# Low weight parts on VectorE, first clips on GpSimd, and the last third products by token halves

## The chip, the core and the metric

The kernel runs on one core of a Trainium2 chip. The metric is the device time of one execution in microseconds (us); lower is better. The engines of the core are named as in the profile: PE is TensorE (matmul), PEld its weight loads, DVE is VectorE, ACT is ScalarE, POOL is GpSimd and SP is SyncE, which only issues DMAs. Each engine takes its own instructions in the order in which the program has them, and waits where a semaphore tells it to.

## The reference

A Mamba-2 scan (batch 4, 8 heads, 768 steps, head dimension 32, state 16) is followed by a SiLU feed-forward block on its output, seen as 3072 tokens of 256 features. With `a` clipped to [1e-6, 1]:

```
for each chunk of 32 steps:            # per batch and head
    cum = cumsum(log a);  L = tril(exp(cum_i - cum_j))
    y   = ((C B^T) * L) x  +  (C state) * exp(cum)
    state = exp(sum log a) * state + sum_j exp(cum_last - cum_j) B_j x_j^T
X = y as (3072, 256)
h = X @ w_in                            # 256 x 2048
out = (h * sigmoid(h)) @ w_out          # 2048 x 256
```

`x`, `a`, `B`, `C` are float32; `w_in` and `w_out` arrive as float64.

## The kernel before

**Units and pairs.** The 3072 tokens are cut into 12 units `u` of 256 tokens (three to a batch), and these into 6 pairs `P` (in the first product `G`) of 512 tokens. The scan of a unit needs decay products (`E`, `P`: scans on DVE from factors that a DMA spreads over the partitions), `B` and `C` turned and weighted (`T`, `ce`, `B`, `C`), matmuls `g0` (C with B), `gd`/`D` (state updates), the mask `M` and the state steps `S` on DVE, `SM` on ACT, and the output matmuls `Y`. Its result is copied out of PSUM by ACT (`X0` for the first two units, `y` for the others).

**The feed-forward block.** Pair 0 uses float32 matmuls: `s` (first product), `si` (SiLU), `n` (second product, 32 of them). Pairs 1 to 5 use float32r, which rounds its operands, and so need three products: a high part `h`, a low part `l` and a third part `d` of both factors. `a` holds the `h` and `l` products of one block `i` of 256 features, `ax` rescales the sum in PSUM, `d` adds the third product, `dg` is the SiLU, `h`, `l`, `e` make the three parts of the result (ACT, DVE, DVE), and the second product takes them as single matmuls, the `f` items, from the list `S2`. Pair `P` has 8 blocks `i`, and per block 12 items: two halves `k`, two output halves `m`, three parts. The sums lie in four PSUM banks `ACC` (`h`+`l` and `d`, for `m` = 0 and 1).

**The weights** come as 16 blocks `n` of 256 columns (0 to 7 of `w_in`, 8 to 15 of `w_out`) as pairs of 32-bit words. ACT makes `u` (size of the high word) and `v` (low word), DVE clips `u` (`w,n,0`, line 292), shifts it (`w,n,1`, line 296) and sets the sign in `v` (`w,n,2`, line 299), POOL adds the two (`W`, line 310). Then come the parts: `H` on ACT (line 314), `Wl`, the low part, which POOL adds out of the high part and the weight (line 319), `Wd` on ACT (line 322), and `We`, an accumulating DMA on POOL's queue (line 326), which adds the low part into the third.

**The order of the work** is written out by hand: `SCHEDULE` is a list of tokens (`name,arguments`) that is emitted from left to right, and each engine gets its share in that order; `SLOTS` lists which buffer each request takes. `z` are matmuls on zeros at the start. The last pair is ended differently from the others: for its last blocks (`i >= LASTI`) the `m = 1` items are held back in `LAST`, `h` and `l` first, the third products (`d`) at the very end. Then `Vt` (line 703) adds the third products to the rest in four token blocks `k`, `ot` (line 715) turns them by matmuls on the identity, two blocks a half, `or` copies each half out of PSUM (ACT, DVE) and `os` (line 726) stores it.

Of the kernel before, what the change touches and what calls it, by code (L numbers as in the profile page):

```python
# [13 lines left out]
ALU = mybir.AluOpType  # L14
# [4 lines left out]
ip,0 ia cs ci ir,3 c1 ch c2 Ln,0,0,0,1 z,1 cI z,1 z,1 Lt,0,1,2,1 Lt,0,1,0,1 zr z,0,6 z,0,6 A z,0,6 z,1 cd lw,2 cP cp  # L19
Lt,0,1,1,1 z,1 z,1 PA,0 z,1 z,1 z,1 pb,0 Lt,0,1,3,1 ab,0,0 T,0,1 ab,0,1 P01,0 Ln,0,0,1,1 ab,1,1 Lx,0,0,0 lw,0 Lx,0,1,0  # L20
PA,1 ce,0,0 v,2 C,0 u,2 z,1 u,0 z,1 z,0,6 Ln,1,0,1,0 E,0,0 Ln,1,1,0,0 E,0,1 E,1,1 Ln,1,0,0,0 ce,0,1 w,0,0 B,0,0 z,0,6
B,0,1 z,0,6 Ln,1,1,1,0 tp,0 tq,0 D,0 g0,0 S,0,0 Lt,3,1,1,0 S,0,1 v,0 pb,1 w,2,0 S,0,2 Lx,1,0,0 M,0,1 M,0,0 Lx,1,1,0
ir,0 ab,1,0 ct co lw,1 w,2,1 w,2,2 SM,0,1 SM,0,0 B,1,1 tp,1 ce,1,1 tq,1 Y,0 ce,1,0 X0,0,0 S,0,3 X0,0,1 E,1,0 P01,1
lw,3 W,2,2,0 W,2,2,1 H,2 u,1 w,0,2 B,1,0 w,0,1 g0,1 v,1 lw,4 D,1 S,1,0 S,1,1 S,1,2 v,3 SM,1,0 M,1,0 s,0,2 M,1,1 w,1,0
SM,1,1 W,0,2,0 ir,1 w,1,2 lw,10 u,3 Lt,3,1,3,0 W,0,2,1 ir,2 w,1,1 s,0,0 si,0,0 C,1 u,4 S,1,3 w,3,0 W,1,2,0 lw,9 lw,8
v,4 w,3,2 W,1,2,1 w,3,1 Y,1 lw,11 X0,1,1 X0,1,0 u,10 s,0,1 w,4,0 Ln,2,1,1,0 H,0 s,1,2 Wl,2 w,4,2 AA,0 Ln,2,0,1,0
si,0,2 si,0,1 s,1,0 u,9 v,10 w,4,1 AD,4 w,9,0 Ln,2,0,0,0 W,3,1,0 w,10,0 v,9 W,4,1,0 si,1,2 H,3 s,1,1 si,1,1 u,8 s,1,4
H,4 si,1,0 Lt,3,1,2,0 v,8 Ln,2,1,0,0 s,0,4 Lx,2,0,0 w,10,1 lw,5 AA,1 v,11 ca La,2,0,0 w,9,1 tp,2 si,1,4 Wl,4 AD,0
w,8,0 w,8,1 w,8,2 Lt,3,1,0,0 La,2,1,0 w,10,2 lw,7 Lx,2,1,0 w,9,2 si,0,4 W,8,1,0 lw,6 w,11,2 W,9,1,0 Lp,2,0 W,10,1,0
u,5 s,1,3 AD,2 Lt,3,0,1,0 s,0,3 n,1 tq,2 si,1,3 H,8 AD,1 v,5 w,5,0 n,1 T,3,1 n,1 ce,2,0 La,3,1,0 E,2,1 La,3,0,0 ce,2,1  # L30
n,1 u,11 w,11,0 n,1 E,2,0 si,0,3 w,11,1 v,7 Wd,4 n,1 Wd,3 B,2 n,1 g0,2 gd,2 w,5,1 b,2,0 b,2,1 n,1 w,5,2 Lt,3,0,3,0 u,6
W,5,1,0 P,2 n,1 Lt,4,1,2,0 M,2,1 s,0,5 Wd,0 n,1 v,6 C,2 ce,3,0 Lt,3,0,2,0 Lt,4,1,0,0 H,1 S,2,0 S,2,1 u,7 w,6,0
Ln,3,0,1,0 W,11,1,0 S,2,2 n,1 H,9 SM,2,0 Lt,3,0,0,0 n,1 M,2,0 w,7,0 SM,2,1 w,7,2 lw,12 E,3,0 Ln,3,0,0,0 w,7,1 Wd,1
ce,3,1 si,0,5 Lt,4,1,3,0 E,3,1 T,3,0 Lx,3,0,0 Y,2 Lp,3,0 n,1 w,6,1 Lx,3,1,0 u,12 y,2,0 W,7,1,0 n,1 s,0,7 y,2,1 H,5
w,6,2 g0,3 w,12,0 B,3 si,0,7 gd,3 W,6,1,0 w,12,1 Lt,4,0,1,0 s,0,6 b,3,0 P,3 AD,3 Wd,2 n,1 M,3,1 Wl,0 lw,13 S,3,0 b,3,1
Wl,5 xh,2 si,0,6 S,3,1 v,12 Ln,4,0,1,0 lw,14 x,2,1 C,3 n,1 Lt,4,0,0,0 Ln,4,0,0,0 u,13 s,1,6 M,3,0 x,2,0 La,4,0,0
w,13,0 S,3,2 v,13 SM,3,0 SM,3,1 We,0 w,12,2 Lt,4,0,2,0 Y,3 si,1,6 y,3,0 La,4,1,0 y,3,1 xh,3 S,3,3 W,12,1,0 La,5,0,0
Wl,3 Lp,4,0 x,3,0 s,1,5 n,1 Wd,5 w,13,2 w,13,1 Lt,4,0,3,0 a,1,0 H,6 si,1,5 n,1 Lt,4,1,1,0 H,7 lw,15 H,12 Wd,8 H,11
H,10 Lx,4,0,0 s,1,7 x,3,1 W,13,1,0 E,4,1 v,14 T,4,1 P,4 Lx,5,0,0 n,1 T,4,0 ax,1,0 Lt,5,1,2,0 d,1,0 Wl,10 Lx,4,1,0
ce,4,0 n,1 Wd,6 C,4 E,4,0 Lx,5,1,0 ce,4,1 n,1 u,14 dg,1,0 w,14,0 g0,4 B,4 gd,4 w,14,2 Wl,11 n,1 b,4,0 M,4,1 b,4,1  # L40
S,4,0 We,2 Lt,5,1,1,0 u,15 S,4,1 S,4,2 w,14,1 h,1,0 SM,4,1 si,1,7 M,4,0 Lt,5,0,3,0 SM,4,0 v,15 Lt,5,1,0,0 e,1,0
La,5,1,0 n,1 Lt,5,1,3,0 W,14,1,0 Wl,9 S,4,3 Wl,1 n,1 Y,4 y,4,0 n,1 We,1 f,1 Lp,5,0 y,4,1 w,15,0 w,15,1 La,6,0,0 w,15,2
Wl,8 We,4 W,15,1,0 Lt,5,0,2,0 xh,4 Lt,5,0,1,0 a,1,2 Lx,6,1,0 Wl,12 a,1,1 n,2 La,6,1,0 ax,1,1 T,5,1 Lt,6,1,0,0 E,5,0
n,1 ce,5,1 n,1 Wd,9 x,4,1 Wd,10 l,1,0 d,1,1 Ln,5,0,0,0 ax,1,2 n,1 We,8 d,1,2 P,5 dg,1,1 H,15 n,1 x,4,0 dg,1,2 We,3 n,1
a,1,4 E,6,0 ce,5,0 a,1,3 H,13 We,9 f,1 Vn,1 H,14 h,1,1 Vn,0 Ln,5,0,1,0 We,10 Wd,11 f,1 E,5,1 f,1 ax,1,4 f,1 ax,1,3 f,2
Lt,6,1,2,0 Wl,14 Lt,5,0,0,0 d,1,4 f,1 d,1,3 T,5,0 f,1 h,1,2 C,5 Lt,6,1,1,0 f,1 Lt,6,0,2,0 f,1 Lt,6,1,3,0 e,1,1 dg,1,4
f,1 Lt,6,0,3,0 Lt,6,0,0,0 Lt,6,0,1,0 f,1 l,1,1 f,1 B,5 dg,1,3 g0,5 T,6,1 gd,5 Wd,7 f,1 M,5,1 We,5 ce,6,0 b,5,0 f,1
h,1,3 Ln,6,0,1,0 f,1 Ln,6,0,0,0 S,5,0 b,5,1 e,1,2 S,5,1 S,5,2 f,1 Wl,7 a,1,5 M,5,0 l,1,2 h,1,4 f,1 Lp,6,0 f,1 ax,1,5
f,1 Lt,7,1,2,0 f,3 Lt,7,1,0,0 P,6 l,1,3 e,1,3 d,1,5 o,0,0,2 f,1 SM,5,1 dg,1,5 f,1 Wl,6 f,1 Wd,12 ce,6,1 We,7 f,2 l,1,4
f,2 SM,5,0 Y,5 T,6,0 Lt,7,1,1,0 f,1 We,11 We,12 f,3 y,5,1 f,1 a,1,7 E,6,1 Lx,6,0,0 Lx,7,0,0 e,1,4 f,2 B,6 f,3  # L50
Ln,7,0,1,0 y,5,0 ax,1,7 f,1 h,1,5 We,6 xh,5 d,1,7 f,2 C,6 dg,1,7 o,0,1,2 f,1 Lt,7,0,2,0 f,1 Wl,15 Wd,15 gd,6
Lt,7,1,3,0 Lx,7,1,0 g0,6 f,2 M,6,1 x,5,0 Wd,14 Wl,13 f,1 x,5,1 f,2 b,6,0 b,6,1 f,1 h,1,7 M,6,0 f,1 l,1,7 a,2,1 ax,2,1
a,1,6 Wd,13 Lp,7,0 S,6,0 d,2,1 f,1 e,1,5 We,13 S,6,1 ax,1,6 f,1 l,1,5 Lt,7,0,1,0 dg,2,1 La,7,1,0 T,7,1 d,1,6 dg,1,6
ce,7,0 f,1 S,6,2 SM,6,0 f,2 Lt,7,0,0,0 SM,6,1 f,2 h,1,6 f,1 Y,6 l,1,6 La,8,0,0 S,6,3 Lt,8,1,0,0 f,3 y,6,0 f,1 e,1,6
O,0,0,2,0,0 ce,7,1 P,7 f,3 y,6,1 We,15 La,7,0,0 xh,6 f,1 O,0,1,2,0,0 Lt,7,0,3,0 a,2,0 f,1 a,2,3 f,2 h,2,1 We,14 f,1
ax,2,0 E,7,0 d,2,0 ax,2,3 f,4 e,1,7 La,8,1,0 Lt,8,1,3,0 f,4 dg,2,0 f,1 E,7,1 f,1 d,2,3 f,1 l,2,1 f,1 x,6,0 Lt,8,1,2,0
a,2,2 f,2 h,2,0 dg,2,3 Ln,7,0,0,0 ax,2,2 f,1 O,0,1,2,3,0 e,2,0 f,4 l,2,0 T,7,0 f,2 Lt,8,0,2,0 B,7 f,1 Va,1,0 f,1 d,2,2
Va,1,1 f,1 Vd,1,0 f,1 Vd,1,1 f,3 dg,2,2 Lt,8,0,3,0 f,1 g0,7 x,6,1 gd,7 b,7,0 f,2 b,7,1 Lt,8,1,1,0 f,1 e,2,1 h,2,2
M,7,0 S,7,0 S,7,1 Ln,8,0,1,0 f,1 S,7,2 f,1 M,7,1 f,1 Ln,8,0,0,0 Lt,8,0,1,0 a,2,4 Lx,8,1,0 ax,2,4 C,7 a,2,5 f,2 T,8,1
ax,2,5 f,1 d,2,4 S,7,3 l,2,2 d,2,5 Lp,8,0 dg,2,4 E,8,0 P,8 SM,7,1 f,1 dg,2,5 f,4 e,2,2 Lt,8,0,0,0 E,8,1 f,2  # L60
O,0,1,2,2,0 f,1 T,8,0 SM,7,0 Lt,9,1,1,0 f,1 Y,7 y,7,1 f,1 h,2,3 f,1 e,2,3 f,1 y,7,0 a,2,7 Lt,9,0,2,0 ax,2,7 a,2,6 f,1
ax,2,6 Lx,8,0,0 Lt,9,0,0,0 Lx,9,0,0 d,2,7 La,9,0,0 f,1 d,2,6 f,1 l,2,3 f,2 ce,8,1 La,9,1,0 f,1 h,2,4 f,2 E,9,1 l,2,4
xh,7 ce,8,0 f,2 dg,2,7 f,4 dg,2,6 f,1 e,2,4 f,1 B,8 f,2 Ln,9,0,0,0 f,1 g0,8 gd,8 f,1 b,8,0 x,7,0 f,2 M,8,1 Lp,9,0
M,8,0 f,1 x,7,1 C,8 f,1 o,1,0,2 f,1 o,1,1,2 O,0,0,2,2,0 b,8,1 Lt,9,0,3,0 S,8,0 Lt,9,1,0,0 a,3,1 f,2 Lt,9,1,3,0
Lt,9,1,2,0 f,1 h,2,5 S,8,1 T,9,1 ce,9,0 ax,3,1 f,1 a,3,0 f,1 e,2,5 ax,3,0 S,8,2 d,3,1 h,2,6 f,1 d,3,0 l,2,5 SM,8,1
Lt,10,1,0,0 dg,3,0 f,3 Lt,9,0,1,0 f,1 l,2,6 f,1 Lt,10,1,3,0 SM,8,0 f,1 e,2,6 E,9,0 P,9 f,1 O,0,0,2,3,0 dg,3,1 f,1
ce,9,1 f,2 Ln,9,0,1,0 Lt,10,1,2,0 f,1 Y,8 y,8,0 f,1 h,3,0 B,9 f,1 O,0,1,2,1,0 f,2 h,2,7 f,1 O,0,0,2,1,0 O,1,0,2,0,0
f,1 h,3,1 l,2,7 O,1,1,2,1,0 y,8,1 Lt,10,1,1,0 e,2,7 C,9 a,3,2 f,3 a,3,3 e,3,0 f,2 ax,3,2 T,10,1 f,1 d,3,2 O,1,1,2,2,0
La,10,1,0 f,2 ax,3,3 xh,8 d,3,3 f,3 l,3,0 x,8,1 f,1 Lp,10,0 Lt,11,1,3,0 f,1 Lx,10,0,0 Lx,9,1,0 f,1 T,9,0 La,10,0,0
dg,3,2 f,1 dg,3,3 f,2 O,1,0,2,3,0 Va,2,0 g0,9 gd,9 f,1 b,9,0 Ln,10,0,0,0 M,9,1 Lt,10,0,0,0 f,1 l,3,1 b,9,1 f,1 a,3,5  # L70
f,1 Lt,11,1,2,0 Va,2,1 f,1 S,9,0 Vd,2,0 M,9,0 f,2 O,1,1,2,0,0 ce,10,1 a,3,4 f,1 O,1,0,2,1,0 Vd,2,1 f,1 o,2,0,2 e,3,1
f,5 ax,3,5 Lt,11,1,0,0 f,1 S,9,1 E,10,1 E,10,0 ce,10,0 Lt,11,1,1,0 ax,3,4 f,1 O,1,1,2,3,0 S,9,2 h,3,3 d,3,4
Ln,10,0,1,0 SM,9,0 SM,9,1 x,8,0 f,1 dg,3,4 f,1 d,3,5 f,1 dg,3,5 O,1,0,2,2,0 f,1 Lt,10,0,2,0 f,5 h,3,2 Y,9 y,9,1
o,2,1,2 Lx,10,1,0 f,1 S,9,3 l,3,2 e,3,2 f,1 Lt,10,0,1,0 f,2 h,3,5 a,3,7 f,3 e,3,3 f,3 O,2,1,2,0,0 h,3,4 La,11,1,0 B,10
l,3,3 l,3,4 f,1 Lt,10,0,3,0 f,1 y,9,0 ax,3,7 d,3,7 T,10,0 f,3 xh,9 dg,3,7 f,2 x,9,0 f,1 Lt,11,0,1,0 f,2 g0,10 h,3,7
gd,10 O,2,0,2,1,0 f,1 b,10,0 f,1 l,3,5 M,10,0 P,10 x,9,1 b,10,1 M,10,1 f,3 S,10,0 f,1 O,2,1,2,2,0 C,10 f,1 a,3,6 a,4,1
# [30 lines left out]
    "raw": """  # L107
0 1 2 3 4 5 6 0 1 2 3 4 0 5 6 3 2 1 4 0 1 5 4 6 3 2 1 0 5 6 4""",
    "hp": """
0 1 2 0 1 2 0 1 2 1 0 2 2 1 0 2 1 2 0 1 2 0 1 1 1 1 1 1 1 2 0 1 0 2 1 2 0 1 2 0 1 2 0""",  # L110
}
PASSED = (0, 1, 2, 3, 4, 5, 6, 7, 8, 9, 10, 11, 12, 13, 14, 15,)
LASTI = 6
# [769 lines left out]
```

## Time and profile before

| | |
|---|---|
| median of 3 runs | 330.02 us (329.69 to 330.54) |
| profiled execution: its time | 329.56 us |
| its span (first to last instruction) | 327.5 us |
| PE busy | 321.0 us, 3081 matmuls |
| DVE busy | 238.4 us |
| ACT busy | 207.7 us |
| POOL busy | 90.2 us |
| granted PE clock, mean | 0.999 |

The span leaves out 2.06 us of the execution's own time. A matmul record is longer than the step from one matmul to the next, because matmuls are pipelined; the steps are told from the starts. Tokens can be followed in the trace one by one, since each engine's instructions come in the order of `SCHEDULE`.

### The profile page before, as it was taken

What the parts mean: (1) busy time and instruction counts of PE and PEld (TensorE: products, weight loads), DVE (VectorE), ACT (ScalarE), POOL (GpSimd) and SP (SyncE); (2) the same over time, 40 slices, a digit from 0 to 9 for tenths busy, and PEclk for the clock granted to TensorE, in tenths of its full rate; (3) what the DMA queues carried; (4) which work ended last, traced back from release to release, by engine and by line L of the source; (5) the groups of instructions that cost most, each with busy time, mean ns of one, the idle gap of its engine ahead of it and who ended that gap; (6) DMA issues with size and microseconds to landing.
All of it is one profiled execution on the core that took longest, in us unless ns stands there. A gap on an engine that the chain in (4) does not pass through costs nothing.

```text
span 327.5 us, 7562 instructions
## 1 busy us (share of the span) xinstructions
PE 321.0 (98%) x3081; PEld 244.3 (75%) x3081; DVE 238.4 (73%) x311; ACT 207.7 (63%) x321; POOL 90.2 (28%) x104
## 2 busy tenths in 40 slices
PE   8999999999999999999999999999999999999995
PEld 3588656665677777877878878878887888888883
DVE  4999999799996955789377769776567554266373
ACT  2888855696498478655566766745856464764441
POOL 6467847658967343210100101010010000000000
PEclk9999999999999999999999999999999999999999
DMA  7999785865888357421603253144001200003102
GB/s 182 167 337 216 201 200 120 207 150 131 149 152 153 57 123 139 103 42 40 139 18 58 69 109 57 47 73 82 2 0 22 38 0 2 0 9 63 18 0 64
DMA packets 95761, 30.64 MB, mean 94 GB/s; under 512 B 80280, under 2 KB 86936, under 8 KB 95728
## 3 DMA queue, kind: packets, MB, share of 16 engines
q1 hardware_dynamic: 90576, 25.38, 35.1%
q0 software_dynamic: 2480, 4.39, 7.4%
q10 hardware_dynamic: 2672, 0.39, 0.7%
q8 instruction: 24, 0.39, 0.5%
q14 instruction: 9, 0.07, 0.1%
HBM read 22.61 MB, written 3.34 MB: 79 GB/s over the span
## 4 chain that ended last, share of the span: by engine, by line
PE 88%; DMA 4%; DVE 4%; issue 1%; ACT 1%; SPq 1%; POOL 0%; DVEq 0%
PE hp L763 29%; PE ga L782 17%; PE gb L782 17%; PE o_ps L763 6%; PE hp L673 4%; PE hp L741 4%; DMA ac<-r4k 2%; PE ga L613 2%; PE ga L553 2%; DMA ab<-az 2%; PE ga L604 1%; PE o_ps L417 1%; PE hp L468 1%; PE gb L604 1%; PE ga L539 1%
## 5 line engine op out<-in xcount | busy, mean ns | idle before, releaser
L763 PE MATMUL hp<-r4k,s2k 128*128 128x512 f32 x400 | 113.3, 394 | 0.0
L763 PEld LDWEIGHTS hp<-r4k,s2k 128*128 128x128 f32 x400 | 74.3, 188 | 16.2 <-issue 0.6
L630 DVE SCALAR_TENSOR_TENSOR r4k<-r4k,r4k 128x1024 fp32r<-128x1024 f32 x40 | 49.1, 1230 | 31.5 <-ACT r4k L809 23.9
L782 PE MATMUL ga<-raw,s2k 128*128 128x512 f32 x240 | 63.0, 398 | 0.0
L633 DVE SCALAR_TENSOR_TENSOR r4k<-r4k,r4k 128x1024 fp32r<-128x1024 f32 x40 | 50.1, 1257 | 16.5 <-ACT r4k L809 10.3
L782 PE MATMUL gb<-raw,s2k 128*128 128x512 f32 x240 | 61.5, 392 | 0.0
L782 PEld LDWEIGHTS ga<-raw,s2k 128*128 128x128 f32 x240 | 44.6, 188 | 12.2 <-issue 1.4
L782 PEld LDWEIGHTS gb<-raw,s2k 128*128 128x128 f32 x240 | 44.8, 188 | 10.4 <-ACT gb L793 0.4
L809 ACT ACTIVATE r4k<-r4k 128x1024 fp32r<-128x1024 f32 x40 | 41.8, 1056 | 2.0 <-DVE r4k L633 1.0
L486 POOL TENSOR_TENSOR BT<-bn,ab 128x256 f32<-128x256 f32 x10 | 10.0, 1000 | 94.3 <-DVE ab L478 49.7
L793 ACT ACTIVATE gb<-gb 128x1024 f32<-128x1024 f32 x20 | 20.2, 1008 | 20.8 <-PE gb L782 20.8
L763 PE MATMUL o_ps<-r4k,s2k 128*128 128x512 f32 x80 | 30.9, 392 | 0.0
L478 DVE TENSOR_TENSOR_SCAN ab<-ab,diag 128x512 f32<-128x512 f32 x20 | 28.3, 1425 | 3.3 <-DMA ab<-az 3.3
L741 PE MATMUL hp<-r4k,s2k 128*128 128x512 f32 x64 | 30.2, 598 | 0.0
L803 ACT ACTIVATE r4k<-ga 128x1024 f32<-128x1024 f32 x20 | 20.5, 1026 | 15.1 <-PE ga L782 14.2
L673 PE MATMUL hp<-r4k,s2k 128*128 128x256 f32 x128 | 29.8, 383 | 0.0
L793 ACT ACTIVATE ga<-ga 128x1024 f32<-128x1024 f32 x20 | 20.2, 1009 | 15.1 <-PE ga L782 15.1
L310 POOL TENSOR_TENSOR s2k<-s2k,s2k 128x512 uint32<-128x512 uint32 (+1 forms) x19 | 23.9, 1266 | 17.7 <-DVE s2k L296 9.9
L673 PEld LDWEIGHTS hp<-r4k,s2k 128*128 128x128 f32 x128 | 23.8, 190 | 5.5 <-issue 1.9
L803 ACT ACTIVATE r4k<-gb 128x1024 f32<-128x1024 f32 x20 | 20.5, 1024 | 9.2 <-PE gb L782 7.4
L319 POOL TENSOR_TENSOR s2k<-s2k,s2k 128x512 fp32r<-128x512 f32 x16 | 23.9, 1538 | 3.8 <-ACT s2k L314 3.8
L741 PEld LDWEIGHTS hp<-r4k,s2k 128*128 128x128 f32 x64 | 11.8, 189 | 9.6 <-issue 7.9
(120 smaller groups left out, 396.6 us busy)
## 6 DMA issues: line engine op xcount, KB each, us to landing
ab<-az SPq DMA_DIRECT2D x20, 256.0 KB
raw<-in_moe_w_in_dram SPq DMA_DIRECT2D x8, 512.0 KB
raw<-in_moe_w_out_dram SPq DMA_DIRECT2D x8, 512.0 KB
s2k<-s2k POOLq DMA_DIRECT2D x16, 256.0 KB, 4.5
out_dram<-r4k SPq DMA_DIRECT2D x44, 64.0 KB
xt<-in_x_dram SPq DMA_DIRECT2D x20, 128.0 KB
pz<-ac SPq DMA_DIRECT2D x10, 130.0 KB
bn<-in_B_dram SPq DMA_DIRECT2D x20, 64.0 KB
```

The lines of the kernel that those rows point to most:

```text
L310: nc.gpsimd.tensor_tensor(out=dst[:, :, fs].bitcast(U32), in0=u[:, :, fs], in1=v[:, :, fs], op=ALU.add)
L319: nc.gpsimd.tensor_tensor(out=t, in0=f32(WK[n, "h"]), in1=WT[n], op=ALU.add)
L478: nc.vector.tensor_tensor_scan(out=o, data0=src, data1=diag.rearrange("p h t -> p (h t)"), initial=0.0, op0=ALU.mult, op1=ALU.add)
L630: nc.vector.scalar_tensor_tensor(out=l, in0=f32(h), scalar=BACK, in1=y, op0=ALU.mult, op1=ALU.add)
L633: nc.vector.scalar_tensor_tensor(out=d, in0=f32(h), scalar=-(BACK + 1.0), in1=y, op0=ALU.mult, op1=ALU.subtract)
L673: nc.tensor.matmul(out=hp[:, i], lhsT=WT[j][:, kc, 128 * i:128 * i + 128], rhs=XM[:, 2 * kc:2 * kc + 2, u], start=(kc == 0), stop=(kc == K ...
L741: nc.tensor.matmul(out=NP["o"][m], lhsT=WT[8 + f // 2][:, f % 2, 128 * m:128 * m + 128], rhs=GT[0, f // 2][:, f % 2], start=(f == 0), stop ...
L763: nc.tensor.matmul(out=ACC[P, 2 * (p == "d") + m], lhsT=WK[8 + f // 2, p][:, f % 2, 128 * m:128 * m + 128], rhs=rhs, start=(f == 0 and p ! ...
L782: nc.tensor.matmul(out=o, lhsT=WK[j, q][:, kc, 128 * i:128 * i + 128], rhs=xs[:, 2 * kc:2 * kc + 2], start=(start and q == "h" and kc == 0 ...
L793: nc.scalar.activation(t, t, AF.Copy, scale=1.0 + Z)
L803: nc.scalar.activation(g, t, AF.Silu, scale=BACK)
L809: nc.scalar.activation(t, GT[G, i], AF.Copy, scale=-LESS * Z)
```

## The change

- `Wl,n` is done by DVE for all 16 weight blocks (`BESIDE`), as a `scalar_tensor_tensor` with a factor of 1.0. POOL did it before.
- The clip `w,n,0` of weight blocks 0, 1 and 2 (`CLIPPED`) is done by POOL. DVE did it before and still does for the other 13.
- `LASTI` is 5: the `m = 1` items of the last three blocks of the last pair are held back, not those of the last two. Their third products run as matmuls of 256 tokens, not 512: first the six for one half of the tokens into a bank of `ga`, then the six for the other half into a bank of `gb` (`s2_late`). The sums of blocks 0 to 4 stay in `ACC`; `Vc` (ACT) copies them to SBUF, `Vb` (DVE) adds the `h`+`l` sum, and `Vt` adds the late bank of the half that it belongs to.
- `SCHEDULE` and `SLOTS` are written anew. The order of tokens shifts throughout by some places on each engine. ACT's dummy SiLU `ct` stands ahead of its other work, so one activation table is loaded where there were two.

```diff
 PASSED = (0, 1, 2, 3, 4, 5, 6, 7, 8, 9, 10, 11, 12, 13, 14, 15,)
-LASTI = 6
+LASTI = 5
+CLIPPED = (0,1,2,)
+BESIDE = (0,1,2,3,4,5,6,7,8,9,10,11,12,13,14,15,)
...
             if what == 0:
                 u = wu[n]
-                nc.vector.tensor_scalar(out=u, in0=u, scalar1=LEAST, scalar2=MOST, op0=ALU.max, op1=ALU.min)
+                engine = nc.gpsimd if n in CLIPPED else nc.vector
+                engine.tensor_scalar(out=u, in0=u, scalar1=LEAST, scalar2=MOST, op0=ALU.max, op1=ALU.min)
                 return
...
             t = WK[n, p] = small([128, 2, WF], FR)
-            nc.gpsimd.tensor_tensor(out=t, in0=f32(WK[n, "h"]), in1=WT[n], op=ALU.add)
+            if n in BESIDE:
+                nc.vector.scalar_tensor_tensor(out=t, in0=f32(WK[n, "h"]), scalar=1.0, in1=WT[n], op0=ALU.mult, op1=ALU.add)
+            else:
+                nc.gpsimd.tensor_tensor(out=t, in0=f32(WK[n, "h"]), in1=WT[n], op=ALU.add)
...
     def f_vt(P, m, k):
-        o, t = (v.rearrange("p (c k t) -> p k c t", c=2, k=4)[:, k] for v in (OUT[P][0][:, m], ACC[P, 2 + m]))
+        o = OUT[P][0][:, m].rearrange("p (c k t) -> p k c t", c=2, k=4)[:, k]
+        t = LATE[k // 2][:, 1, 0:256].rearrange("p (c k t) -> p k c t", c=2, k=2)[:, k % 2]
...
-                         start=(f == 0 and p != "l"), stop=(f == NF - 1 and p != "h"), skip_group_check=True)
+                         start=(f == 0 and p != "l"), skip_group_check=True,
+                         stop=(f == (2 * LASTI if (P, m, p) == (NPAIR - 1, 1, "d") else NF) - 1 and p != "h"))
+
+    def s2_late(P, i, k, half):
+        f = 2 * i + k
...
+        nc.tensor.matmul(out=LATE[half][:, 1, 0:256].rearrange("p (c t) -> p c t", c=2),
+                         lhsT=WK[8 + f // 2, "d"][:, f % 2, 128:256],
+                         rhs=DT[P, i][:, k].rearrange("p (c u t) -> p c u t", c=2, u=2)[:, :, half],
+                         start=(f == 2 * LASTI), stop=(f == NF - 1), skip_group_check=True)
...
+    def f_vc(P, m):
+        nc.scalar.activation(OUT[P][0][:, m], ACC[P, 2 + m], AF.Copy, scale=BACK)
+
+    def f_vb(P, m):
+        o = OUT[P][0][:, m]
+        nc.vector.scalar_tensor_tensor(out=o, in0=ACC[P, m], scalar=BACK * (1.0 + Z), in1=o, op0=ALU.mult, op1=ALU.add)
...
         S2.extend(items((0,), "hld"))
-        LAST.append((items((1,), "hl"), items((1,), "d")))
+        LAST.append((items((1,), "hl"), [[partial(s2_late, G, i, k, half) for k in range(2)] for half in range(2)]))
         if i == NF // 2 - 1:
-            for v in range(2):
+            for t in LAST:
+                S2.extend(t[0])
+            for half in range(2):
                 for t in LAST:
-                    S2.extend(t[v])
+                    S2.extend(t[1][half])
```

Token orders that the prediction speaks of (other tokens left out):

```
before: ... Y,0 X0,0,0 X0,0,1 ... g0,1 D,1 ...       ... y,3,0 y,3,1 xh,3 ... x,3,0 ... a,1,0 ... ax,1,0 ... d,1,0
after:  ... Y,0 D,1 X0,0,0 X0,0,1 ... g0,1 ...       ... y,3,0 y,3,1 v,14 xh,3 ... x,3,0 ... a,1,0 ... ax,1,0 ... d,1,0
before (end): Va,5,0 f,1 Vd,5,0 f,5 o,5,0,2 f,3 Va,5,1 f,4 Vt,5,1,0 Vt,5,1,1 ot,5,1,0 ... Vt,5,1,2 Vt,5,1,3 ot,5,1,1 ...
after (end):  Va,5,0 ... Vc,5,1 f,10 Vb,5,1 Vt,5,1,1 f,3 Vt,5,1,0 ... Vt,5,1,2 Vt,5,1,3 ot,5,1,0 ot,5,1,1 ...
```

## The prediction

> **What bounds the kernel now.** I read the page's busy line and the chain that ended last, then the busy time by windows of 5 us to find where PE is not full, then PE's, DVE's and POOL's timelines around those places.
>
> ```profile
> PE 321.0 (98%) x3081; PEld 244.3 (75%) x3081; DVE 238.4 (73%) x311; ACT 207.7 (63%) x321; POOL 90.2 (28%) x104
> ...
> PE 88%; DMA 4%; DVE 4%; issue 1%; ACT 1%; SPq 1%; POOL 0%; DVEq 0%
> ```
>
> PE sets the time. Since the change keeps PE's work, it can gain only where PE waits, at the head, or behind the last matmul. The windows (length, then busy time of PE, PEld, DVE, ACT, POOL, granted clock) show the waits:
>
> ```profile
> 10.00:15.00 5.00, 4.80 (x148) 3.18 (x152) 4.88 (x12) 3.80 (x10) 1.19 (x4) 1.00 0.86 119
> 15.00:20.00 5.00, 4.53 (x129) 3.70 (x116) 4.86 (x11) 4.06 (x11) 3.19 (x5) 1.00 1.03 322
> ...
> 60.00:65.00 5.00, 4.28 (x101) 3.32 (x100) 3.46 (x9) 2.82 (x8) 2.46 (x3) 1.00 0.72 162
> ```
>
> All other windows from 10 to 320 us have PE full. So 1.4 us are to be had there (0.2 + 0.47 + 0.72), and no more. The two larger ones on PE's timeline, with what released them:
>
> ```profile
> 16.29 0.43 PE L553 MATMUL ga<-ce,bh 32*64 32x128 f32 x4 [0.47 <-ACT r4k L643]
> ...
> 63.59 0.27 PE L613 MATMUL ga<-cw,sm 32*64 32x64 f32 x2 [0.72 <-ACT sm L591]
> ```
>
> The first is `g0,1` waiting for the copy `X0`; the second is the end of `Y,3` waiting for `SM,3`. ACT is named there, but `SM,3,0` started 0.04 us after DVE's `S,3,2` ended at 62.77, so DVE was late. Why, DVE's and POOL's timelines and POOL's group say:
>
> ```profile
> 55.75 3.42 DVE L458 TENSOR_TENSOR_SCAN pfx<-pz,one 128x260 f32<-128x260 f32 x1
> ```
> ```profile
> 56.09 2.51 POOL L319 TENSOR_TENSOR s2k<-s2k,s2k 128x512 fp32r<-128x512 f32 x2
> ```
> ```profile
> L319 POOL TENSOR_TENSOR s2k<-s2k,s2k 128x512 fp32r<-128x512 f32 x16 | 23.9, 1538 | 3.8 <-ACT s2k L314 3.8
> L292 DVE TENSOR_SCALAR s2k<-s2k 128x512 f32<-128x512 f32 x16 | 10.5, 659 | 0.2 <-ACT s2k L283 0.2
> ```
>
> The scan has a median of 0.69 us; it took 3.42 while two `Wl` adds ran on POOL. Summing every DVE instruction's excess over its usual duration gives 26.0 us, of which 9.6 lie mostly beside `Wl` (3.8 before 62 us) and 9.3 beside `W` (line 310). DVE is full to 60 us, so these count.
>
> **Part 1: `Wl` on DVE, three clips on POOL.** Nothing in this trace shows `Wl` on DVE. Its nearest row is DVE's line 633 on the same shape and types (128x512, float32r out of two float32 operands): 0.68 us. So DVE gets 16 x 0.68 = +10.9 and loses three undisturbed clips, 3 x 0.41 = -1.2: +9.7 of its own work, against 9.6 of stretch that should go with POOL's adds. In total a draw, so the places decide. POOL loses 23.9 and gets three clips at about 0.67 (line 429, a POOL operation with a scalar on 48x512).
>
> *The clips.* They add a wait: DVE's shift `w,2,1` now stands behind POOL's `w,2,0`, with `S,0,2`, `M,0` and so `Y,0` (0.41 to spare) queued behind it. In the trace of before `u,2` was there at 9.31 and POOL's `B,0,1` ended at 10.84; a clip of 0.67 behind it ends at 11.5, and DVE reaches the shift about 12.3: 0. At 1.0 each (two thirds of `Wl`'s 1.54, for one operand less), the dearer bound, it is still there at 11.9, but `PA,1`, which stands behind both clips, moves from 12.6 to 13.3 and with it `pb,1` and `P01,1`: up to +0.5. I take 0.
>
> *At `Y,3`.* The last thing that it needs was `S,3,2`, and is now `M,3,0`. By usual durations, DVE's own work up to it grows by 1.1 (five `Wl` for 3.4, less 1.2, less what is now behind it). With 3.8 of stretch saved it ends 2.7 earlier, near 60.1, and PE is there at about 61.7: the 0.72 go. They stay if less than 2.2 of the 3.8 are saved.
>
> *At `Y,4`.* DVE's own work up to `M,4,1` is now 3.9 longer than before up to `M,4,0`, which ended at 78.27 (seven `Wl` are ahead). Less 0.45 that DVE idled: 81.7 without any saving, 77.9 with 3.8. PE is there at 78.6 + 1.1 (matmuls that move ahead of it) - 0.35 - 0.72 + 0.4 = 79.0. No wait, with a margin of 1.1.
>
> *The order on ACT.* `xh,3` now stands behind `v,14`, whose step in the trace of before is 0.56 us. The chain `Y,3`, `y,3`, `xh,3`, `x,3,0`, `a,1,0` had no slack (`x,3,0` ended at 66.51, as `a,1,0` began). It loses 0.56, and gets 0.22 back because `x,3,0` took 0.90 beside a `Wl` and should take 0.68: between 0 (if `v,14` finds a gap, since `Y,3`'s halves are copied apart) and 0.6; I take **+0.4**.
>
> *Elsewhere.* `We`, the third parts and `Lp,6` shift on POOL's and SP's queues (`lw,6` is behind `Lp,2`; `AD,2` is far later, ahead of `Lp,6`). Their users come several us later by the order; POOL's lighter load hides it. If that cover failed, `s,0,6` would wait for its weights.
>
> **Part 2: the head.** `D,1` (32 matmuls, 17.18 to 17.56) now stands before `g0,1`, in the 0.47 wait for `X0`: **-0.35**, at most -0.47, and 0 if `B,1,0` on POOL comes late: it stands behind two clips, and needs `E,1,0`, which ended at 16.30 and is about 1.1 earlier in DVE's new order, so that I put it at 15.6 against 15.9 for `D,1`. The one activation table load less saves 1.28 us on ACT, which then waits for DVE and DMAs as before: 0.
>
> **Part 3: the tail.** The last matmul starts at 322.46; behind it run these on DVE and PE:
>
> ```profile
> 322.96 0.89 DVE L703 SCALAR_TENSOR_TENSOR r4k<-o_ps,r4k 128x128 f32<-128x128 f32 x4 [0.95 <-PE o_ps L763]
> ```
>
> Four `Vt`, 0.22 each. Two of them now need only the first half's bank and run under the second half's matmuls: **-0.45**. Twelve matmuls of 256 columns stand for six of 512. The step of a float32r 512 is 0.227 us, so I take half, 0.113, and no change. No row shows such a 256. The lower bound is 0.109, at which PE's 128-column transposes follow one another; the upper is the float32 256 of line 673, 0.2155: 12 x 0.2155 - 6 x 0.227 = +1.2. `Vc` and `Vb` (about 0.6 and 0.7) run in idle time of ACT and DVE ahead of the last matmul; if `Vb` were late, the two early `Vt` would move back behind, +0.45.
>
> **Sum.** -0.35 - 0.72 + 0.4 - 0.45 = -1.1 on the profiled execution's 329.56: 328.4. That execution lies 0.46 under the median of the runs, 330.02; so **328.9**.
>
> **Rivals.**
>
> *Nothing is saved (slower).* 9.3 us of DVE's stretch lie beside POOL's `W`, which stays. If a DVE instruction that no longer meets a `Wl` meets a `W` instead, `Y,4` waits for `M,4,1` from 79.7 to 81.7: +2.0 - 0.45 = +1.55, median 331.6. If besides two of the seven `Wl` (POOL is on `W` about 0.3 of the time) meet a `W` as line 299 did at 34.16 us (1.76 for 0.68), 2.2 more: 333.7. It turns slower from less than 0.6 of 3.8 saved. For it: DVE is full there, and stretch follows POOL's activity. Against: the scan's 2.7 us came from two `Wl` in a row, which cannot recur.
>
> *Part is given back.* Each new add can itself be held by a running `W`: 7 adds x 0.3 x half of 1.5 us = 1.6, so 2.2 of 3.8 are left. Then `M,4,1` ends near 79.5, 0.5 past 79.0, and the forecast becomes 329.4; with 1.9 saved, or a piece of the 0.72 kept as well, 329.7 to 330.5.
>
> The Trainium skill, page "SBUF — State Buffer", section "SBUF: two separate sides", says that VectorE and GpSimd share a pair of ports as an exclusive lock for a whole instruction, and that a VectorE operation with two SBUF inputs takes it. The new adds have two SBUF inputs, so by that rule moving `Wl` trades a hold for a hold, and this rival is its outcome. The trace agrees for single rows (3.42 beside 2.51 of POOL), not for all: a line 633 at 60.36 took its 0.68.
>
> *Halves cost as float32 does.* +1.2: 330.1.
>
> **Chances.** A measurement of this kernel can tell about 0.3%, 1 us: faster is under 329.0. Forecast 0.50 (0.43 faster, 0.07 within, as the +0.4 and -0.35 may each miss); part given back 0.16 (0.01, 0.10, 0.05 slower, where later order adds a wait); halves 0.05 (within); nothing saved 0.29 (slower). Together faster 0.44, same 0.22, slower 0.34. The range: down to 327.9 (no give-back, all of 0.47 and some of the 0.2), up to 332.0, half of the slower rival; the likeliest case alone spans 327.9 to 329.8.
>
> **What would show it.** Right: DVE's new add near 0.68 us, `P,3` back at 0.7, no gap of PE at 63 us nor at `Y,4`, a gap of 0.3 to 0.4 before `a,1,0`, none over 0.15 at `g0,1`; late 256-column matmuls 0.113 apart; two line 703 instructions behind the last matmul. Wrong: the add at 1.2 or more on average, DVE's total stretch near 26 still, PE waiting for `M` or `x` between 60 and 80 us, or PE losing time in a window that was full.

## The result and the profile after

The changed kernel takes 332.19 us (median of 12 runs, 331.03 to 333.42), the kernel before, run beside it, 329.68: a ratio of 1.0073 (95% interval 1.0058 to 1.0088), 2.4 us slower. The forecast was 328.9. The profiled execution took 331.03, with a span of 329.3 us against 327.5: 1.8 us more, and where these lie can be read. What an execution takes outside its span differs too, by 0.33 us: 2.00 to 2.13 us in every run of the kernel before, 1.66 to 1.79 in every run of a changed one. No term of the sum stands for that, its cause is not known, and it is in every ratio below.

The busy line and the chain that ended last: POOL has gone from nothing to 2% of the chain.

```profile
PE 321.0 (97%) x3087; PEld 245.0 (74%) x3087; DVE 234.1 (71%) x325; ACT 206.3 (63%) x320; POOL 75.1 (23%) x91
...
PE 95%; POOL 2%; issue 1%; ACT 0%; DVE 0%; ACTq 0%; POOLq 0%
```

The same windows as before, and the one after them (busy time of PE first). At 60 us PE is now full, as forecast. The loss is at 10 to 15 us (2.81 for 4.80), and 0.63 more follow at 20 to 25, where PE had been full:

```profile
10.00:15.00 5.00, 2.81 (x73) 1.34 (x69) 4.21 (x9) 1.35 (x4) 4.68 (x4) 1.00 0.91 113
...
15.00:20.00 5.00, 4.55 (x161) 3.50 (x162) 4.53 (x10) 3.39 (x10) 4.47 (x8) 1.00 1.03 361
...
20.00:25.00 5.00, 4.37 (x106) 3.48 (x109) 4.32 (x9) 3.17 (x7) 3.48 (x3) 1.00 1.09 322
...
60.00:65.00 5.00, 5.00 (x81) 3.65 (x81) 4.96 (x11) 3.85 (x9) 1.65 (x1) 1.00 1.00 229
```

PE's timeline names both waits. The first is `pb,1`, the spread of `PA,1`; the second is within `Y,1`, and has no releaser ("issue", time in which the profile shows nothing that PE waits for):

```profile
15.35 0.70 PE L452 MATMUL hp<-s2k,s2k 8*128 8x260 f32 x2 [2.34 <-POOL s2k L447]
...
24.30 0.34 PE L610 MATMUL gb<-ab,s2k 64*32 64x64 f32 x14 [0.63 <-issue]
```

POOL's timeline says why `PA,1` (line 447) is late, and the groups give the sizes: the clip (line 295) takes 1.916 us on POOL, not 0.67, and two stand ahead of `PA,1`. The low part (line 323) takes 0.825 on DVE.

```profile
11.01 3.81 POOL L295 TENSOR_SCALAR s2k<-s2k 128x512 f32<-128x512 f32 x2
14.90 0.39 POOL L447 TENSOR_SCALAR s2k<-s2k 8x256 f32<-8x256 f32 x1
```
```profile
L323 DVE SCALAR_TENSOR_TENSOR s2k<-s2k,s2k 128x512 fp32r<-128x512 f32 x16 | 13.2, 825 | 0.0
...
L295 POOL TENSOR_SCALAR s2k<-s2k 128x512 f32<-128x512 f32 x3 | 5.7, 1916 | 0.2
```

Starts on PE of single tokens give the sum (us):

| | before | after | difference |
|---|---|---|---|
| `s,0,2` | 17.56 | 19.29 | +1.73 |
| `s,0,1` | 22.62 | 25.20 | +2.58 (the stop in `Y,1`) |
| `Y,3` | 62.01 | 64.38 | +2.37 |
| `a,1,0` | 66.39 | 67.96 | +1.57 (the 0.72 wait gone) |
| last `f` matmul | 322.46 | 324.48 | +2.02 |
| last turning matmuls | 323.70 | 325.34 | +1.64 |

### The profile page after: what moved, and what is told of

The parts are those of the page before. It is cut to its first block, busy times and chain, and to the rows that moved or that the text cites. A ratio compares the mean times of both kernels' runs of the same rounds, so it can differ in the third digit from the quotient of the medians.

```text
span 329.3 us, 7578 instructions
## 1 busy us (share of the span) xinstructions
PE 321.0 (97%) x3087; PEld 245.0 (74%) x3087; DVE 234.1 (71%) x325; ACT 206.3 (63%) x320; POOL 75.1 (23%) x91
## 4 chain that ended last, share of the span: by engine, by line
PE 95%; POOL 2%; issue 1%; ACT 0%; DVE 0%; ACTq 0%; POOLq 0%
PE hp L767 28%; PE ga L806 17%; PE gb L806 16%; PE hp L745 9%; PE hp L679 9%; PE o_ps L767 5%; PE ga L559 2%; PE ga L619 2%; PE ga L610 2%; PE gb L610 1%; PE ga L545 1%; PE o_ps L423 1%; POOL s2k L295 1%; PE hp L474 1%; PE gb L559 1%
## 5 line engine op out<-in xcount | busy, mean ns | idle before, releaser
L767 PE MATMUL o_ps<-r4k,s2k 128*128 128x512 f32 x74 | 29.1, 394 | 0.0
L313 POOL TENSOR_TENSOR s2k<-s2k,s2k 128x512 uint32<-128x512 uint32 (+1 forms) x19 | 23.4, 1239 | 16.5 <-DVE s2k L299 11.4
L484 DVE TENSOR_TENSOR_SCAN ab<-ab,diag 128x512 f32<-128x512 f32 x20 | 24.7, 1240 | 2.3 <-DMA ab<-az 2.3
L332 POOL DMA_DIRECT2D s2k<-s2k x16 | 14.1, 1012 | 31.1 <-DVE s2k L323 18.9
```

What stands on the lines that cost most here:

```text
L313: nc.gpsimd.tensor_tensor(out=dst[:, :, fs].bitcast(U32), in0=u[:, :, fs], in1=v[:, :, fs], op=ALU.add)
L332: nc.gpsimd.dma_start(out=f32(WK[n, p]).rearrange("p k f -> p (k f)"), in_=other.rearrange("p k f -> p (k f)"), accum_op=ALU.add)
L484: nc.vector.tensor_tensor_scan(out=o, data0=src, data1=diag.rearrange("p h t -> p (h t)"), initial=0.0, op0=ALU.mult, op1=ALU.add)
L767: nc.tensor.matmul(out=ACC[P, 2 * (p == "d") + m], lhsT=WK[8 + f // 2, p][:, f % 2, 128 * m:128 * m + 128], rhs=rhs, start=(f == 0 and p ! ...
```

## Experiments

Ratios are to the kernel before, run on the same chip.

**The clips back on VectorE** (`clips_dve`).

```diff
-CLIPPED = (0,1,2,)
+CLIPPED = ()
```

> The changed kernel with the three clips back on VectorE, its order of tokens kept. Theory (the clips): on GpSimd one clip takes 1.92 us where 0.67 was assumed; PA,1 stands behind two of them, and PE waits 2.34 us for it before pb,1. Then that wait goes, DVE gets 3 x 0.41 back, and the time falls by 2.0 to 2.4 us against the changed kernel's 332.2, to about 330; no PE wait over 0.5 us between 10 and 16 us. Rival (VectorE full): the time is lost because the Wl adds overload VectorE; then the clips back on it make it worse, 332.5 to 333. Second rival (clock): 1.2 us of the median come from a granted clock near 0.995 in most runs of the changed kernel, which is not caused by the PE wait: then the median stays above 331 with the wait gone.

Measured: 331.10 us, ratio 1.0027 (1.0003 to 1.0050). The 2.34 went, but not all of it was gained: two clips now stand ahead of `E,1,1` on DVE, which started at 12.24 instead of 10.57, and PE waited 0.86 for it at `ab,1,0`. A median above 331 is also what the clock rival asks for; `z_fill` below bears on that. The stop in `Y,1` stayed:

```profile
13.51 1.12 PE L474 MATMUL hp<-s2k,s2k 128*128 128x512 f32 x2 [0.86 <-DVE ab L484]
...
24.00 0.34 PE L610 MATMUL gb<-ab,s2k 64*32 64x64 f32 x14 [1.05 <-issue]
```

So VectorE was no place to put the clips back in this order; they have to be short on POOL.

**`PA,1` ahead of the clips** (`pa_first`).

```diff
-... D,0 w,2,0 ... w,2,1 PA,1 S,0,2 ...
+... D,0 PA,1 w,2,0 ... w,2,1 S,0,2 ...
```

> The changed kernel with PA,1 ahead of the three clips on GpSimd and nothing else changed. Theory (the place of PA,1): the PE wait of 2.34 us before pb,1 goes, since PA,1 needs no clip; what is next late is the chain clip 1.92 + 1.92, W,2 and B,1, which D,1 and g0,1 need: 0.5 to 1.5 us of PE waits come back there, so the time falls by 1 to 2 us, to 330.2 to 331.2. Rival (the length of the clips alone): everything behind them on GpSimd is late anyway, no gain over 0.5 us.

Measured: 332.80, ratio 1.0065 (1.0043 to 1.0087): no gain, as the rival had it. `PA,1` ran at 10.96, but DVE's queue took its place: `w,2,1` waited 1.15 us for the clip and began at 13.39, `S,0,2` stands behind it and ended at 14.4, and `pb,1` needs the bank that `S,0,2` reads:

```profile
14.56 0.67 PE L452 MATMUL hp<-s2k,s2k 8*128 8x260 f32 x2 [1.61 <-DVE st L589]
```

So it is the clip's length, which makes PE wait by way of `PA,1` or by way of DVE's queue.

**What a clip costs on GpSimd** (`pool_alone`, then `pool_forms`): late in the kernel, on a dead buffer (one whose values nobody needs any more). In the first run the buffer has 1024 columns, where the expectation says 512, and its clips are minimum first with bounds 1 and 1e-6.

```diff
+        if i == 1:
+            nc.gpsimd.tensor_scalar(out=a, in0=a, scalar1=LEAST, scalar2=MOST, op0=ALU.max, op1=ALU.min)
+        if i == 2:
+            nc.gpsimd.tensor_scalar(out=a, in0=a, scalar1=MOST, scalar2=LEAST, op0=ALU.min, op1=ALU.max)
+        ...
```

> The changed kernel with clips on VectorE, and late, where GpSimd idles, three times seven operations on GpSimd on a dead buffer, to time them by themselves: clip (two operations) on 128x512, on 48x512, one operation on 128x512, clip on 128x256, an add of two operands on 128x512, clip on 16x512 and on 64x512. If the time goes by the number of partitions, 48x512 takes about 0.7 and 128x512 1.9; if by the second operation, one operation on 128x512 takes about 1.0 to 1.2 and 48x512 takes about 1.9 too, which the 0.67 of AA speaks against; if by VectorE's work beside it, the clip on 128x512 takes 0.7 here.

Measured, the shortest of three each (the longest of these clips took 1.90): minimum then maximum 1.03 us on 128x1024, 1.04 on 48x1024 and 1.03 on 16x1024, so the number of partitions makes no difference here. Minimum alone took 2.78, more than both operations together. None of the three readings had that.

> The changed kernel with clips on VectorE, and late, where GpSimd has nothing else, four times six operations on it, all 128x512 on a dead buffer: the kernel's clip (maximum with the lower bound, then minimum with the upper), the same with minimum first, maximum first with the bounds 1e-6 and 1, minimum first with these, maximum alone, an add of two operands. In the run of pool_alone the shortest clip with minimum first took 1.03 us on 128x1024 and 1.03 on 16x1024, minimum alone 2.78. Theory (the order of the two operations decides): maximum first about 1.8 to 1.9 whatever the bounds, minimum first about 0.52 to 0.6. Rival (the values or VectorE beside it): all four clips alike at about 0.55 here, and the 1.92 of the head come from VectorE's instructions beside them.

Line by line, the kernel's clip, minimum first, maximum first with bounds 1e-6 and 1, minimum first with these, maximum alone, an add (shortest/median/longest ns):

```profile
L880 POOL TENSOR_SCALAR ab<-ab x4: 1922/2088/2777, 248.9 to 280.2; 128x512 f32<-128x512 f32 x4
...
L882 POOL TENSOR_SCALAR ab<-ab x4: 615/616/819, 250.9 to 282.2; 128x512 f32<-128x512 f32 x4
...
L884 POOL TENSOR_SCALAR ab<-ab x4: 1917/1930/2771, 251.6 to 282.9; 128x512 f32<-128x512 f32 x4
...
L886 POOL TENSOR_SCALAR ab<-ab x4: 615/1300/1683, 253.6 to 284.9; 128x512 f32<-128x512 f32 x4
...
L888 POOL TENSOR_SCALAR ab<-ab x4: 1491/1814/2342, 255.4 to 285.6; 128x512 f32<-128x512 f32 x4
...
L890 POOL TENSOR_TENSOR ab<-ab,ab x4: 1288/1292/2335, 257.3 to 287.1; 128x512 f32<-128x512 f32 x4
```

The shortest of each four count; the longer ones mostly ran beside VectorE's instructions. The order of the two operations decides: 0.615 us with minimum first, 1.92 with maximum first, whatever the bounds.

**Minimum first** (`min_first`, and with `PA,1` ahead, `min_first_pa`).

```diff
-  engine.tensor_scalar(out=u, in0=u, scalar1=LEAST, scalar2=MOST, op0=ALU.max, op1=ALU.min)
+  nc.gpsimd.tensor_scalar(out=u, in0=u, scalar1=MOST, scalar2=LEAST, op0=ALU.min, op1=ALU.max)
```

> The changed kernel with GpSimd's three clips as minimum, then maximum (the same values). If the order decides, the clip takes 0.55 to 0.7 as the prediction assumed, PA,1 ends near 12.6 us instead of 15.3, pb,1 waits at most 0.3 us instead of 2.34, and the time falls by 2 to 3.5 us against 332.2, to 328.7 to 330.2; the PE gap without a releaser at about 24 us may stay (0.6 to 1.3). If VectorE beside them is the cause, clips stay at 1.9 and the time stays at 332.

Measured: 329.02, ratio 0.9968 (0.9951 to 0.9985): faster than the kernel before by 0.3%, about 1 us, of which 0.33 lie outside the span; and 3.2 us below the changed kernel, by two operations swapped. Its profile (span 327.3) names no PE wait from 8 to 100 us; the stop in `Y,1` is gone too:

```profile
11.78 1.19 POOL L295 TENSOR_SCALAR s2k<-s2k 128x512 f32<-128x512 f32 x2
```
```profile
10.00:15.00 5.00, 4.96 (x95) 2.74 (x93) 4.89 (x10) 1.68 (x5) 4.05 (x8) 1.00 0.90 107
```

> As min_first, with PA,1 ahead of the clips on GpSimd. If the place of PA,1 matters only through the clips' length, this is within 0.5 us of min_first. If pb,1 is still late behind two short clips, it is up to 0.6 faster.

Measured: 329.51, ratio 0.9990 (0.9962 to 1.0017): within 0.5 us, as if the place did not matter once the clips are short.

**Low parts back on GpSimd** (`wl_pool`), in the new order, to be compared with `clips_dve`.

```diff
-CLIPPED = (0,1,2,)
-BESIDE = (0,1,2,3,4,5,6,7,8,9,10,11,12,13,14,15,)
+CLIPPED = ()
+BESIDE = ()
```

> The changed kernel with both moves undone: low parts on GpSimd and clips on VectorE, in the new order of tokens. Theory (saving is real): the traces show DVE's excess over usual durations at 11.4 us with Wl on VectorE against 26.0 with Wl on GpSimd; so with Wl back on GpSimd DVE is late for M,3,0 or M,4,1 and the time is 1 to 3 us above that of the changed kernel with the clips alone undone. Rival (a draw): VectorE's own 10.9 us more cancel the saving, and the two are within 0.5 us.

Measured: 337.71, ratio 1.0214 (1.0184 to 1.0245), 6.6 us above `clips_dve`, more than twice what was expected. DVE's excess over usual durations is 32.9 us here, 15.0 of it beside `Wl`, against 13.4 in `clips_dve`. DVE is late for `M,4,1`, as expected, and for `M,5,1` too, and PE waits for both; `M,3,0` cost nothing (`a,1,0` started at 68.05, in `clips_dve` at 68.01):

```profile
83.33 0.35 PE L610 MATMUL gb<-ab,xt 64*32 64x64 f32 x16 [1.16 <-DVE ab L574]
...
109.30 2.09 PE L806 MATMUL gb<-raw,s2k 128*128 128x512 f32 x8 [2.35 <-DVE ab L574]
```

And `Wl` itself is held up beside DVE, at 1.99 us instead of the 1.54 of before:

```profile
L325 POOL TENSOR_TENSOR s2k<-s2k,s2k 128x512 fp32r<-128x512 f32 x16 | 30.4, 1990 | 0.0
```

The 6.6 us are the price in this order of tokens, which was made for `Wl` on VectorE.

**Low parts on VectorE in the old order** (`b_wl_dve`): the kernel before with that one line changed.

```diff
-  nc.gpsimd.tensor_tensor(out=t, in0=f32(WK[n, "h"]), in1=WT[n], op=ALU.add)
+  nc.vector.scalar_tensor_tensor(out=t, in0=f32(WK[n, "h"]), scalar=1.0, in1=WT[n], op0=ALU.mult, op1=ALU.add)
```

> The kernel before with all Wl on VectorE, nothing else changed: the order of tokens is the one made for Wl on GpSimd. Theory (saving is real, but the order must take it up): DVE's excess over usual durations falls from 26 to 11 to 14 us while its own work grows by 10.9, so PE's 0.72 wait in Y,3 goes or halves, and the time is within 1 us of the kernel before, 329 to 331. Rival (VectorE is overloaded): the added work makes M and S late at Y,2 to Y,4, and the time is 2 us or more above.

Measured: 329.23, ratio 0.9997 (0.9956 to 1.0038). The excess fell from 26.0 to 15.5, and PE's 0.72 wait at `Y,3` was gone (`S,3,2`, which `Y,3` had waited for, ended at 60.83 instead of 62.77, and `a,1,0` started at 65.36 instead of 66.39). The window of 60 to 65 us, with PE 4.28 before:

```profile
60.00:65.00 5.00, 5.00 (x106) 4.15 (x105) 2.65 (x7) 3.74 (x10) 1.84 (x1) 1.00 0.75 166
```

So VectorE is not overloaded; but there is no gain in time that these runs can tell either.

**PE kept busy in the wait** (`z_fill`): nine matmuls on zeros ahead of `pb,1`.

```diff
+z,9
 pb,1
```

> The changed kernel with nine matmuls on zeros (about 1.9 us of PE) put into PE's wait before pb,1, nothing else changed. Clock theory: runs of the changed kernel show a mean granted clock of 0.988 to 0.999, where the kernel before shows 0.997 to 1.000, because PE idles 2.34 us in the head and then gets half the clock for a while; then the wait, and so the profiled span, stay within 0.3 us, but the clock is back at 0.997 to 1.000 and the median falls by about 1 us, to 331.0 to 331.4. Rival (the clock has another cause, or the scatter has): the median stays at 332.2 and the clocks near 0.995.

Measured: 332.19, ratio 1.0055 (1.0028 to 1.0081). The mean granted clocks came back to 0.997 to 1.000 in all runs but one, and the median did not move. So nothing speaks for the clock theory, by which the 1.2 us between the changed kernel's profiled execution and its median are lost to PE's idling before `pb,1`. It is not refuted either, since the runs go from 330.19 to 335.78 and the interval still holds the 331.0 to 331.4 that it asked for. What the lower means came from stays open.

**Weight loads out of the way** (`loads_late`, on `clips_dve`; and `min_first_loads`, on `min_first`).

```diff
-... W,0,2,1 lw,10 ir,1 ... s,0,2 lw,9 u,3 ... Y,1 ... X0,1,0
+... W,0,2,1 ir,1 ... s,0,2 u,3 ... Y,1 ... lw,10 lw,9 X0,1,0
```

> clips_dve with two weight loads of 512 KB (lw,10 and lw,9) moved from about 17 to 21 us to behind Y,1. In the changed kernel and in clips_dve PE stops for 0.6 to 1.3 us within Y,1, at the same instruction in each, with no releaser; 1.3 to 1.4 us ahead of its going on, a 16 KB packet of the instruction queue ends. In the kernel before and in min_first that packet starts at 18.4 and 18.6 us, and there is no stop; where it starts at 20.8 to 22.9 there is one. Theory (instructions come late because weight loads fill the DMA engines): with two loads less in that stretch the packet starts by 20 us and the stop shrinks to under 0.4 us. Rival (the packet is asked for when PE reaches a certain instruction): the packet stays at 21 to 22 us and the stop at 0.8 to 1.2.

Measured: 331.06, ratio 1.0049 (1.0027 to 1.0072). This profile did as the theory says: the packet started at 20.0 us instead of 21.7, while PE was at most 0.25 us earlier (`Y,1` at 21.98 against 22.21), and the stop was gone. PE's window of 20 to 25 us in `clips_dve` and here:

```profile
20.00:25.00 5.00, 3.95 (x108) 3.09 (x107) 4.97 (x11) 3.00 (x7) 1.75 (x3) 1.00 1.04 343
```
```profile
20.00:25.00 5.00, 5.00 (x113) 4.16 (x112) 4.93 (x11) 4.00 (x9) 1.73 (x2) 1.00 1.04 350
```

The profiled execution took 329.52, but the median of five runs was that of `clips_dve`; nothing of it is seen in the time, and the next run speaks against the theory.

> min_first with the two weight loads lw,10 and lw,9 behind Y,1, as in loads_late. In loads_late's profile the instruction packet started at 20.0 instead of 21.7 us and PE's stop in Y,1 was gone. If late instructions are a part of the slower runs of min_first (those in which PE comes to full clock late, as in the profiles of min_first_pa and full_late with stops of 1.2 and 1.0 us), the median falls by 0.2 to 0.5 us against min_first's 329.0, and fewer runs lie over 330. Rival (the weights of blocks 9 and 10 are then late, or the slower runs have another cause): 329.0 or more, with the same scatter.

Measured: 329.22, ratio 0.9976 (0.9962 to 0.9991), 328.24 to 330.88: no gain on `min_first`. Both beat the kernel before. In its profile PE stops in `Y,1`, where `min_first`, with the loads in their old place, does not:

```profile
22.69 0.34 PE L612 MATMUL gb<-ab,s2k 64*32 64x64 f32 x14 [0.94 <-issue]
```

The packet started at 20.4 us, in `min_first` at 18.6. So with the two loads moved there is one profile without the stop and one with it, and the theory of the weight loads is not borne out.

**The tail at full width** (`full_late`, on `min_first`).

```diff
-        nc.tensor.matmul(out=LATE[half][:, 1, 0:256]..., rhs=DT[P, i][:, k]...[:, :, half],
+        if half == 1:
+            return
+        nc.tensor.matmul(out=LATE[half][:, 1], ..., rhs=DT[P, i][:, k],
```

> min_first with the held-back third products as six matmuls of 512 tokens into one bank, as before the change, so that all four Vt wait for the last of them. Theory (the tail's term): halves let two Vt of 0.22 us run under PE's last matmuls and cost 12 x 0.119 - 6 x 0.227 = 0.07 us more of PE; so from the start of the last f matmul less its own step to the start of the last turning matmul, this kernel takes 0.3 to 0.4 us more than min_first in the trace, and about as much more time. Rival (the tail is bound by the copies and the store behind the turns): no difference over 0.1 us in the span behind the last f matmul.

Measured: 329.96, ratio 1.0010 (0.9984 to 1.0037). In the trace the stretch from the first late matmul to the last store's issue is 3.64 us, in `min_first` 3.11: halves gain 0.5. From the start of the last `f` matmul less its own step to the last turning matmul, the measure that the expectation names, it is 1.98 us for 1.15: 0.8, twice what was expected. In time the medians, taken on different chips, lie 0.9 us apart, with intervals of the ratios that touch; the trace decides. DVE's rows here and in `min_first` (four `Vt` behind the last matmul, or two):

```profile
325.74 0.89 DVE L712 SCALAR_TENSOR_TENSOR r4k<-ga,r4k 128x128 f32<-128x128 f32 x4 [0.60 <-PE ga L782]
```
```profile
322.20 0.49 DVE L712 SCALAR_TENSOR_TENSOR r4k<-ga,r4k 128x128 f32<-128x128 f32 x2
...
322.76 0.49 DVE L712 SCALAR_TENSOR_TENSOR r4k<-gb,r4k 128x128 f32<-128x128 f32 x2
```

## Why the prediction was wrong

The step that failed is one term of the sum: the clip on POOL, taken at 0.67 us with 1.0 as the dearer bound, and at 0 in the sum. It took 1.92. The row that it came from, line 429, is a clip too, but with minimum first; the kernel's has maximum first, which no row of POOL in the trace of before showed, and which is three times as long. The way in which it would hurt had been named: `PA,1` behind both clips, then `pb,1`. At 1.0 this was +0.5; at 1.92 it was 2.34. No rival, no chance and no part of the range stood for a clip dearer than 1.0.

With the order of the two operations alone put right, the kernel takes 329.02, where 328.9 was forecast. That they agree this well is partly luck. Against the profile of before, `min_first`'s has `Y,0` 0.59 us later (PE came to full clock 1.3 us later there; whether that is all of it was not tried), gains 0.38 in the head, 0.21 from there to `Y,3` and 0.80 from `Y,3` to `a,1,0`, where the sum had 0.72 less 0.4; then it loses 0.79 up to the last `f` matmul, for which the sum had nothing, and gains 0.22 behind it, where the sum had 0.45. The span is 0.23 shorter, and 0.33 lie outside it. The gains in the head and at the wait of `Y,3` are as the prediction had them; the other terms miss, and their errors cancel.

Point by point:

- **Head, -0.35.** Right: from `Y,0` to `s,0,2` 2.72 us for 3.11, so -0.39.
- **`Y,3`, -0.72.** Right: from `Y,3` to `s,1,5` 1.29 us for 2.09.
- **`Wl` on VectorE, a draw with stretch saved.** Right in kind: the excess fell from 26.0 to 11.4 us, and `b_wl_dve` shows the same in the old order (15.5). The size of the add, 0.68, was 0.825 in the mean: 12 of 16 near 0.68, four between 1.09 and 1.76, held beside POOL.
- **The rival "nothing is saved".** It gave 331.6 to 333.7, and the time fell into that stretch by another way. At `Y,4`, where it had its wait, PE does not wait for `M,4,1`, and DVE had time to spare there: it idled 2.94 us ahead of `S,4,0`, waiting for ACT (the line below). The rule of the Trainium skill (page "SBUF — State Buffer", section "SBUF: two separate sides") agrees with four held adds, each of which ran beside an operation of POOL that had begun before it and ended 0.55 to 0.56 us behind that one's end, and with `wl_pool`, where each engine is slow beside the other (15.0 us of DVE's excess beside `Wl`, and `Wl` at 1.99). It did not decide: the held adds lost 2.3 us in all, where the adds on POOL had held DVE for 9.6. The row that the prediction set against the rule, line 633 at 60.36, ran beside no arithmetic of POOL, which only issued a DMA then, so it doesn't speak against it.

```profile
77.85 0.68 DVE L589 SCALAR_TENSOR_TENSOR st<-st,pfx,bxs 128x64 f32<-128x64 f32 x2 [2.94 <-ACT bxs L568]
```

- **Given back, +0.4 at `a,1,0`.** Wrong: `s,1,5` to `a,1,0` is 2.29 us in both, no wait. `xh,3` did come 0.38 later behind `s,1,5`, but the chain had slack: `x,3,0` ended 0.28 us behind the start of `a,1,0` (0.12 before), and is needed only by the low products of `a,1,0`, from its third matmul on, at 68.82 us.
- **Tail, -0.45.** From the last `f` matmul to the last store's issue 1.79 us for 2.26, -0.47; less 0.11, by which a shorter last matmul starts later, and less 0.07 for twelve halves at 0.119 each (0.113 assumed): -0.29. The end of the span gains less, since from the issue of the last store to it are 3.05 us instead of 2.79; the last store now goes out on SP's queue and not on ACT's, and whether that is why was not tried.
- **Not foreseen: the stop in `Y,1`.** From `s,0,2` to `s,0,1` 5.91 us for 5.06, +0.85, of which the stop is 0.63. It belongs to the packet of the instruction queue (see the last section), not to the clip: `clips_dve` has it without the 2.34 us wait. A late head isn't the cause either: `min_first_loads` has the earliest `Y,1` of all profiles (21.01 us) and the stop, `full_late` the latest (24.23) and no stop there. What sets the packet's start is open.
- **Not foreseen: +0.45 between `a,1,0` and the last `f` matmul.** The halves are 0.18 of it, as in the tail above. About 0.4 are lost ahead of `Y,4`, where the step from the matmul ahead of it is 0.73 us; ahead of `Y,5` it is 0.32. The profile names no releaser, and it is not `M,4,1`: in `wl_pool`, where that ended 1.45 us after `Y,4` began, the step is 0.72. The cause is open.

## What to carry to other kernels

A row is a price for an instruction only if the operations in it are the same in the same order; where a new form stands ahead of something that the critical engine needs, time it alone first, on a dead buffer in the engine's idle time. An operation moved to an idle engine is moved into that engine's queue: list what stands behind it there, and what in the old queue now waits for it. When a change bundles several edits, one mis-sized term can hide the gains of the others: here 2.34 us of wait hid the 1.2 gained in the head and at `Y,3`.

## What was not expected of the hardware

- On GpSimd, minimum then maximum is cheaper (0.615 us on 128x512) than maximum then minimum (1.92), and than maximum alone (1.49).
- PE can stop for 0.4 to 1.3 us in the middle of a run of like matmuls, with no releaser. The stop in `Y,1` lies at the same matmul in every profile that has it, so far as its records are complete, and ends 1.2 to 1.5 us behind a 16 KB packet of the instruction queue. In the nine profiles with the stop this packet started at most 1.2 us ahead of `Y,1` (21.93 and 22.94 us in the changed kernel's), in the five without it about 2 us or more ahead (18.43 and 21.21 before; 20.02 and 21.98 in `loads_late`). In one of these five, `full_late`, PE had stopped for 0.96 us in `D,1`, at 19.48 us, behind an earlier packet. That the instructions come late is the reading that fits these figures; what delays a packet was not found.
- PE does not come to full speed at the same time in each execution. The six matmuls on zeros at 3.8 us took 1.80 us in the changed kernel's profile, and 2.74 in `min_first`'s; in the first, their step falls from 0.427 to 0.216 us on the way. The recorded full clock begins at 4.5 us in the first, 5.7 before, 7.0 in `min_first`, 10.7 in `min_first_pa` (span 330.9).

```profile
3.76 1.80 PE L423 MATMUL o_ps<-s2k 128*128 128x512 bf16 x6
```
```profile
3.75 2.74 PE L425 MATMUL o_ps<-s2k 128*128 128x512 bf16 x6
```

The Trainium skill, page "TensorE: Matmul & The Clock Gate", section "Part 1: The HAM clock gate (the "warmup" mystery)", says that the array is at half clock until a free-running window of about 3.4 us was busy, so that the ramp differs from run to run. The traces agree: the full clock lasts 317.44, 320.85, 324.27 or 327.68 us in the profiles, steps of 3.41. So two profiles may differ by about 1 us for this alone, as the six matmuls above do (0.94). The changed kernel's profiled execution, early at full clock (4.5 us), was also its shortest run. That this is what spreads the other runs was not tried.
